# Retention and a two-layer block on one core: w1 in eight pieces, half runs of the first product, and another order of the early work

## The chip, the cores and the metric

The kernel runs on one core of one Trainium2 chip. The time is device microseconds of that core, the median of several executions. A profiled execution of its own gives the trace; its time, its span and the median are told apart below. TensorE is called PE here, its weight loads PEld, VectorE DVE, ScalarE ACT, GpSimd POOL and SyncE SP.

## The reference, cut to what matters

```python
# q, k, v: (B, H, S, D) = (4, 8, 768, 64)
gamma = 1.0 - 2.0 ** (-5.0 - np.arange(H))
for t in range(S):
    state = gamma[None, :, None, None] * state + np.einsum('bhd,bhe->bhde', k[:, :, t], v[:, :, t])
    y[:, :, t] = 1 / np.sqrt(D) * np.einsum('bhd,bhde->bhe', q[:, :, t], state)
x = y.transpose(0, 2, 1, 3).reshape(B, S, H * D)           # 4 x 768 x 512
xn = (x - mean(x)) / np.sqrt(var(x) + 1e-06) * g_ln
out = x + np.maximum(xn @ w_ch1, 0.0) @ w_ch2              # 512 -> 2048 -> 512
```

## The kernel before, in words

There are 24 tiles of 128 tokens: the first chunk of each of the four batches (tiles 0 to 3), then chunks 1 to 5 batch by batch (tiles 4 to 23). Per tile the kernel forms the masked product of q and k (`vis`, `am`), the attention output (`py`), a state that passes from chunk to chunk (`vg`, `pd`, `pb`), the normalisation (`bn`, `xn`, `xc`, `sq`, `rs`), a transpose of the normalised tile (`tx`, `ex`), the first product with relu (`m`, `r`), the second product (`z`), and scale, residual and store (`ad`, `st`). The first product runs over groups of tiles: tiles 0 to 7 each alone, then four groups of two, then two groups of four. A group's product is cut into runs that fill one PSUM bank; `m0_4` is the run of group 0 that begins at hidden block 4 of 16. For a group of one tile such a run is 16 matmuls of 128 columns and needs one quarter of w1; `r0_4` evacuates it with relu.

Nothing schedules this at run time. The list `ORDER` (lines 36 to 96) is the program order, token by token, and each engine works through its own tokens strictly in that order. The letter after a slash names the engine that evacuates or issues the DMA (A is ACT, D is DVE, S is SP), the names after two slashes the PSUM banks: X0 to X3, Y0, Y1, M and PD. An instruction waits until its inputs are there and until its bank or buffer has been read by its last reader; everything behind it on its engine waits too.

The tokens that the steps below touch, with their lines:

- `k1`, `q1`, `v1` (line 337) load one tile of k, q or v and cast it to bf16; `W0` to `W3` (line 356) load a quarter of w1, `Z0` to `Z3` (line 361) a quarter of w2. All of these are issued by POOL, in order, in one queue. Tile 0's k and q come by ACT and SP in float32 (`hk0a` and so on, line 345) and are cast on ACT or DVE (`hkc0`, `hqc0a`, `hqc0b`, line 244/246).
- `iota`, `pos` (lines 265, 270) on POOL, then `small`, `consts`, `zero` (state cleared, line 316), `idn`, `arg`, `lmul`, `cm`, `mask` (line 303) on DVE and `vsc`, `qsc`, `gch` on ACT make the constants.
- `tk2`, `tq2` (line 372) transpose k and q of a tile on PE (tiles 0 to 6), `ek2` (line 244/246) and `eq2` (line 386) evacuate them; from tile 7 on `tr7` transposes by a DMA on SP's queue (line 380) and `eq7` scales.
- `vis2` (line 395), `am2a`, `am2b` (line 408, DVE), `py2` (line 423), `bn2` (lines 431, 432), `xn2` (line 441), `tx2` (line 486), `ex2`.
- `gb` (line 328) broadcasts the gain on PE, `gl` (line 332) takes it to SBUF.
- `warm8_1` (line 564) is 8 matmuls of 512 columns and 1 of 128 on zeros: PE work that computes nothing.

Of the kernel before, what the change touches and what calls it, by code (L numbers as in the profile page):

```python
# [48 lines left out]
ek6/A eq6 r3_12/A pb6 vg6/ vis6//X2,X1 z1_0//M am6a Z2 am6b m4_8//X2 ex5/D Z3 r4_8/A r4_12/A
vg7/ m1_12//X1 py6//Y0 bn6 k9 xn6 rs2 pd6 m5_8//X0 q9 rs4 pb7 rs1 m5_0//X3 tx6//Y1 r5_8/A q8 eq7  # L50
ex6/D m5_4//X2 r5_0/A k8 vg1/ xc6 r1_12/A m5_12//X3 pd7 r5_4/D v8 sq5 vis7//X0,X2 r5_12/D
m6_12//X1 am7b am7a v9 k10 z1_1 pb8 py7 m6_8//X2 bn7 m6_0//X3 z1_2 rs0 xn7a xn7b z1_3 tr9 xc7b
r6_8/A xc7a pd1 tr8 tx7//Y0 z0_0//Y1 ex7/A gv8 ad1 gq8 gk8 z2_0//Y0 k11 gk10 m7_0//X2 z2_1 gk9
q10 q11 gv9 eq9 rs5 rs3 pb9 r7_0/A r6_12/A r6_0/A z2_2 z0_1 gq9 v11 v10 z0_2 vg9/ z0_3 k12 z2_3
ad0 tr10 gq10 z3_0//M v12 gk11 st0/A ad2 z3_1 tr11 eq8 q13 vis8//X2,X1,X3,X0 z3_2 am8b am8a gv10
vg10/ gv11 z3_3 am9a am9b py8 m7_12//X1 bn8 m7_4//X3 ad3 q12 py9 pd9 bn9 gk12 k13 m6_4//X0
z4_0//M xn9a xn8a xn9b gv12 z4_1 xn8b q14 gq11 pb10 z4_2 k15 ex8/S xc9a r7_12/A eq10 z4_3 k14
r7_4/A xc8b sq7 ex9/S vg11/ ad4 pd10 m7_8//X3 gq12 tr12 r7_8/A z5_0//M gq13 v14 pb11 eq11 st1/A
xc8a xc9b z5_1 r6_4/A vg12/ tr13 z5_2 gq14 vg2/ gk13 vis10//X1,X2,X3,X0 am10a z5_3 pd11 am10b
gk15 v13 q15 m8_4//X1 ad5 m8_14//X2 am11a am11b v15 z6_0//M sq6 pb12 gk14 py10 py11 vg14/ bn11  # L60
# [587 lines left out]
```

## Time and profile before

| what | value |
|---|---|
| median of 3 executions | 213.27 us (212.48 to 214.36) |
| profiled execution: its time | 212.35 us |
| profiled execution: its span | 210.5 us |
| mean granted PE clock | 1.00 |
| DVE busy / ACT busy / POOL busy | 127.7 / 76.9 / 96.5 us |
| POOL's load queue (software), share of 16 DMA engines | 84.6% |

The span runs from the first to the last instruction; 1.85 us of the execution's time lie outside it. A row of the timeline gives start, duration, engine, line, operation, output and inputs, and in brackets how long the engine had been idle and what ended that. A row of the chain of waits gives start and duration of one piece of the chain that ended last. PE's busy share must be read with care: matmuls are pipelined, their ends are modelled, and the zero matmuls of line 564 count as busy.

### The profile page before, as it was taken

What the parts mean: (1) busy time and instruction counts of PE and PEld (TensorE: products, weight loads), DVE (VectorE), ACT (ScalarE), POOL (GpSimd) and SP (SyncE); (2) the same over time, 40 slices, a digit from 0 to 9 for tenths busy, and PEclk for the clock granted to TensorE, in tenths of its full rate; (3) what the DMA queues carried; (4) which work ended last, traced back from release to release, by engine and by line L of the source; (5) the groups of instructions that cost most, each with busy time, mean ns of one, the idle gap of its engine ahead of it and who ended that gap; (6) DMA issues with size and microseconds to landing.
All of it is one profiled execution on the core that took longest, in us unless ns stands there. A gap on an engine that the chain in (4) does not pass through costs nothing.

```text
span 210.5 us, 4985 instructions
## 1 busy us (share of the span) xinstructions
PE 204.3 (97%) x2031; PEld 131.8 (63%) x2031; DVE 127.7 (61%) x297; ACT 76.9 (37%) x168; POOL 96.5 (46%) x145
## 2 busy tenths in 40 slices
PE   7898999999999999999999999999999999999994
PEld 2467999897548667676587686475545444444443
DVE  4797889587248878578695566868948402110023
ACT  6265653642400334515237124314281522346000
POOL 8996593495597797780587449500000000000000
PEclk9999999999999999999999999999999999999999
DMA  9999999999999999999999999996032400015005
GB/s 127 172 181 180 163 195 167 125 172 161 159 121 190 123 178 138 150 118 188 225 145 172 170 166 110 137 108 149 1 104 100 101 0 3 0 50 201 0 3 199
DMA packets 109946, 27.11 MB, mean 129 GB/s; under 512 B 102625, under 2 KB 106977, under 8 KB 109922
## 3 DMA queue, kind: packets, MB, share of 16 engines
q0 software_dynamic: 77024, 13.37, 84.6%
q1 hardware_dynamic: 28242, 6.85, 24.0%
q10 hardware_dynamic: 4656, 6.56, 9.7%
q8 instruction: 16, 0.26, 0.5%
q14 instruction: 8, 0.07, 0.1%
HBM read 27.30 MB, written 6.29 MB: 160 GB/s over the span
## 4 chain that ended last, share of the span: by engine, by line
PE 89%; DVE 8%; ACT 1%; issue 1%; DVEq 0%; ACTq 0%
PE X L520 38%; PE M L543 25%; PE Y L543 9%; PE PD L543 4%; PE X L395 3%; PE Y L423 3%; PE PD L465 2%; PE PD L564 2%; DVE trq L386 2%; DVE asb L408 2%; DVE xn L441 1%; PE Y L401 1%; DVE mask L303 1%; PE Y L372 1%; DVE bns L431 1%
## 5 line engine op out<-in xcount | busy, mean ns | idle before, releaser
L520 PE MATMUL X<-xnt,w 128*128 128x128 bf16 (+2 forms) x896 | 93.9, 257 | 0.0
L531 ACT ACTIVATE h<-X 128x512 bf16<-128x512 f32 x89 | 51.2, 602 | 80.6 <-PE X L520 68.7
L520 PEld LDWEIGHTS <-w 128*128 128x128 bf16 x896 | 66.1, 98 | 20.5 <-issue 0.2
L543 PE MATMUL M<-w,h 128*128 128x512 bf16 x256 | 61.5, 379 | 0.0
L543 PEld LDWEIGHTS <-h 128*128 128x128 bf16 x400 | 37.3, 98 | 37.9
L408 DVE TENSOR_TENSOR asb<-X,mask 128x512 bf16<-128x512 f32 x48 | 30.6, 684 | 11.1 <-PE X L395 10.8
L457 POOL TENSOR_TENSOR vg<-v,vsc 128x512 bf16<-128x512 bf16 x20 | 21.3, 1069 | 9.7 <-DMA v<-in_v_dram 8.6
L550 DVE SCALAR_TENSOR_TENSOR osb<-M,rstd,x_all 128x512 f32<-128x512 f32 x16 | 11.9, 746 | 20.4 <-PE M L543 20.0
L447 ACT CAST x_all<-Y 128x256 bf16<-128x256 f32 (+1 forms) x39 | 14.3, 410 | 26.4 <-DVE xn L441 26.4
L337 POOL DMA_DIRECT2D v<-in_v_dram x24 | 21.8, 910 | 3.7 <-DMA w<-in_moe_w_ch_dram 2.5
L431 DVE BATCH_NORM_STATS2 bns<-Y 128x6 f32<-128x256 f32 (+1 forms) x39 | 16.3, 455 | 9.2 <-PE Y L423 9.0
L543 PE MATMUL Y<-w,h 128*128 128x512 bf16 (+1 forms) x96 | 21.8, 370 | 0.0
L441 DVE SCALAR_TENSOR_TENSOR xn<-Y,mv,gb 128x256 bf16<-128x256 f32 (+1 forms) x39 | 18.7, 513 | 1.2 <-PE Y L423 0.6
L475 DVE TENSOR_TENSOR state<-PD,gch 64x256 bf16<-64x256 f32 x40 | 16.6, 415 | 0.6 <-PE PD L465 0.3
L337 POOL DMA_DIRECT2D qk<-in_q_dram x17 | 15.2, 895 | 1.1 <-issue 1.1
L337 POOL DMA_DIRECT2D qk<-in_k_dram x17 | 15.3, 898 | 0.9 <-issue 0.7
L550 DVE SCALAR_TENSOR_TENSOR osb<-PD,rstd,x_all 128x512 f32<-128x512 f32 (+1 forms) x3 | 1.9, 618 | 20.1 <-PE PD L543 20.1
L386 DVE TENSOR_TENSOR trq<-tr,qsc 128x512 bf16<-128x512 bf16 x17 | 10.1, 597 | 3.6 <-DMA tr<-qk 3.4
L366 POOL COPY scrap<-qk 1x1 bf16<-1x1 bf16 x28 | 5.5, 195 | 11.5 <-DMA qk<-in_k_dram 9.7
L564 PE MATMUL PD<-zeros 128*128 128x512 bf16 (+1 forms) x33 | 9.0, 410 | 1.2 <-DVE zeros L250 1.2
L423 PEld LDWEIGHTS <-asb 128*128 128x128 bf16 x192 | 8.0, 98 | 3.5 <-DVE asb L408 1.6
L543 PE MATMUL PD<-w,h 128*128 128x512 bf16 (+1 forms) x48 | 8.8, 326 | 0.0
(75 smaller groups left out, 131.8 us busy)
## 6 DMA issues: line engine op xcount, KB each, us to landing
out_dram<-osb ACTq DMA_DIRECT2D x23, 256.0 KB, 2.4
w<-in_moe_w_ch_dram POOLq DMA_DIRECT2D x8, 512.0 KB, 9.2
v<-in_v_dram POOLq DMA_DIRECT2D x24, 128.0 KB, 6.6
qk<-in_k_dram POOLq DMA_DIRECT2D x17, 128.0 KB, 6.7
qk<-in_q_dram POOLq DMA_DIRECT2D x17, 128.0 KB, 5.5
k<-in_k_dram POOLq DMA_DIRECT2D x6, 128.0 KB, 8.2
q<-in_q_dram POOLq DMA_DIRECT2D x6, 128.0 KB, 7.8
tr<-qk SPq DMA_TRANSPOSE x17, 5.5
```

The costliest lines, as they stand in the source:

```text
L337: nc.gpsimd.dma_start(out=dst, in_=tok[kind][TILES[t]])
L386: nc.vector.tensor_tensor(out=slot(trq, t), in0=x, in1=qsc, op=ALU.mult)
L408: nc.vector.tensor_tensor(out=slot(asb, t)[:, :, par, :], in0=bank(("pa", t, par)).rearrange("p (i t) -> p i t", t=P), in1=mask.rearrange( ...
L423: nc.tensor.matmul(dst, lhsT=slot(asb, t)[:, h // 2, h % 2, :], rhs=v_of(t)[:, h, :], start=(not late and n == H and h == 0), stop=(h >= H ...
L431: nc.vector.bn_stats(out=bns[:, t, i, :], in_=x)
L441: nc.vector.scalar_tensor_tensor(out=dst, in0=src, scalar=mv[:, t, 0:1], in1=g, op0=ALU.subtract, op1=ALU.mult)
L447: nc.scalar.copy(out=dst, in_=src)
L457: nc.gpsimd.tensor_tensor(out=slot(vgs, chunk(t)), in0=v_of(t), in1=vsc[:, c, :].unsqueeze(2).to_broadcast([P, H, D]), op=ALU.mult)
L475: nc.vector.tensor_tensor(out=slot(state, chunk(t) - 1)[o, :, o], in0=pd[o, :, o], in1=gch[o, c - 1, :].unsqueeze(2).to_broadcast([D, NPAI ...
L520: nc.tensor.matmul(bank(("mm", g, ho))[:, j * n * P:(j + 1) * n * P], lhsT=w1[:, ko, (ho + j) * P:(ho + j + 1) * P], rhs=x[:, x0:x0 + n, k ...
L531: nc.scalar.activation(out=dst, in_=src, func=AF.Relu)
L543: nc.tensor.matmul(bank(("m2", t, piece))[:, 0:hi - lo], lhsT=slot(h1, t // 4)[:, ho, t % 4 * P:(t % 4 + 1) * P], rhs=w2[:, ho, lo:hi], st ...
```

## The change

Three things change. `W` takes a half: w1 arrives in eight DMAs of 256 columns (`W0b`, `W0a` and so on) in place of four of 512. `m` takes a half: for tiles 0 to 7 a run of 16 matmuls is emitted as two of 8 that write the two halves of the same bank, at places of their own in the order; the evacuation stays one. And `ORDER` is a new list from the first token to the last. In its early part `q1`, `k1` go ahead of `iota`, `pos`; `zero` and `mask` come earlier; nine loads of k, q and v in place of four go ahead of the first piece of w1; the attention of tiles 0 to 3 goes ahead of the first product; 13 wide zero matmuls (`warm8_1`, `warm1_3`, `warm3_1`, `warm1_2`) stand in place of 22 wide ones; some evacuations change between ACT and DVE (`ek0`, `ek1`, `ek4`, `ek5`, `ek6`, `ex7`, `r0_4`, `r3_0`, `r5_0`, `r1_12` to DVE; `r0_0`, `ex4`, `ex6`, `r5_12` to ACT). The `late` variable in `vis` gives the same start flags as before for the visits that are in use.

```diff
            'osb': 6}}
 
 ORDER = """
-qsc v1 hkc0/A gch hqc0a/D W0 warm8_1 tk0//Y0 hqc0b/A k2 ek0/A warm1_1 tq0//Y1 eq0 q2 mask
-warm1_3 vis0//X1,X2 gb//X3 W1 am0b vg0/ am0a gl v2 warm3_2 tq1//Y1 py0//M tk1//Y0 eq1 ek1/A k3
-bn0 sqt warm3_1 vis1//X3,X0 q3 xn0 v3 am1a xc0 warm2_3 tx0//Y0 am1b ex0/A W2 zero warm3_0 py1//M
-warm1_0 tk2//Y0 pd0 k4 bn1 ek2/A tq2//Y1 q4 m0_0//X3 xn1 eq2 r0_0/D vis2//X1,X2 tx1//Y0 am2a
-am2b m0_4//X0 v4 xc1 ex1/A py2//Y1 k5 r0_4/A m1_4//X1 bn2 q5 tk3//Y0 m1_0//X2 xn2 ek3/A v5
-r1_4/A tq3//M tx2//Y0 xc2 W3 eq3 ex2/D r1_0/A vis3//X0,X1 m2_4//X3 am3a am3b m2_0//X0 pb4 v7
-py3//Y1 r2_0/A sq0 m0_8//X2 bn3 Z0 r2_4/A tk4//M m1_8//X1 xn3 vg4/ k6 ek4/A r0_8/A xc3 tq4//M
-tx3//Y0 eq4 m2_8//X0 r1_8/D ex3/A vg5/ q6 vis4//X2,X3 r2_8/A am4a am4b m3_4//X1 tk5//Y1 tq5//M
-r3_4/D ek5/A pd4 py4//Y0 eq5 k7 m3_0//X0 bn4 q7 vis5//X1,X3 r3_0/A xn4 m3_8//X2 v6 tx4//M
-m0_12//X0 am5b am5a xc4 Z1 sq1 pb5 m2_12//X1 ex4/D py5//Y1 r2_12/D m4_0//X3 bn5 r0_12/A sq4 sq3
-m4_4//X1 xn5 m3_12//X0 r4_0/D xc5 r4_4/A tk6//M pd5 sq2 tx5//Y1 tq6//Y0 tr7 m4_12//X3 r3_8/A
-ek6/A eq6 r3_12/A pb6 vg6/ vis6//X2,X1 z1_0//M am6a Z2 am6b m4_8//X2 ex5/D Z3 r4_8/A r4_12/A
...
-m8_10//X0 r8_6/A rs8 ex10/S eq12 xn11a xc11a vg15/ sq9 xc10a xc11b pb13 eq13 rs6 xc10b z6_3
...
-vis12//X2,X3,X1,X0 q17 v17 gv16 z7_2 am12a gv15 am13a am13b am12b pb14 k18 z7_3 m9_0//X1 ad7
...
-z11_3 gv20 r10_12/A m11_10//X1 vg20/ xn16b ad11 pd19 gq21 r11_10/A z12_0//M m10_14//X0 eq18 tr21
-vg21/ pb20 xn17a eq19 xn17b vg22/ z12_1 r10_14/A xc16b z12_2 sq11 xc16a xc17a xc17b z12_3 k23
-v23 vis18//X3,X0,X1,X2 ad12 ex17/S ex16/S tr22 pd20 am18b z13_0//M am18a z13_1 am19a py18 z13_2
...
-pb21 eq20 ex19/S sq12 xc19a z14_3 tr23 vis20//X1,X2,X0,X3 ad14 pd21 am21a z15_0//M z15_1 eq22
...
-z22_2 z23_0//Y1 z22_3 z20_0//PD z20_1 z20_2 z20_3 z21_3 ad20 ad22 z23_1 st20/A ad21 z23_2 st22/A
-z23_3 st21/A z23b_0//PD ad23 z23b_1 z23b_2 z23b_3 st23/A ad23b st23b/A
+hk0b/A hk0a/S q1 consts small hq0b/A hq0a/S grow table zero touch k1 iota pos v0 q2 k2 idn lmul
+arg cm vsc hkc0/A warm8_1 tk0//Y0 mask hqc0a/D k3 hqc0b/A qsc warm1_3 tq0//Y1 v1 v2 q3 vg0/
+ek0/D gch eq0 warm3_1 tq1//M vis0//X2,X3 eq1 gb//X1 am0b am0a tk1//M sqt gl py0//Y0 ek1/D bn0
+warm1_2 tq2//Y1 W0b eq2 vis1//X1,X0 pd0 W0a xn0 sq0 tk2//Y1 W1a am1b tk3//M ek2/A ek3/A am1a v3
+vis2//X2,X0 xc0 am2b am2a tx0//M W1b py1//Y0 ex0/A k4 bn1 py2//M tq3//Y1 q4 eq3 xn1 vis3//X1,X0
+W2b m0_0b//X3 bn2 tx1//Y1 W2a ex1/A rs0 m0_0a k5 r0_0/A sq1 m1_0b//X2 xn2 am3b am3a sq2 xc2
+tx2//Y1 m1_0a v4 m1_4a//X0 r1_0/A xc1 ex2/D py3//M q5 m2_4a//X1 m2_0a//X3 bn3 m2_0b r2_0/A W3b
+xn3 m2_4b m1_4b rs1 pb4 xc3 sq3 r1_4/A W3a tk4//Y1 m0_4b//X3 ek4/D q6 tq4//Y0 r2_4/A m0_4a eq4
+tx3//M r0_4/D vis4//X2,X0 ex3/A v5 m2_8b//X1 am4a m1_8b//X3 am4b m3_0a//X2 m3_0b k6 m1_8a r3_0/D
+m2_8a tk5//Y1 r1_8/D m0_8b//X2 q7 r2_8/A ek5/D py4//Y0 m3_8a//X3 vg4/ v6 k7 bn4 tq5//M m3_8b eq5
+m0_8a xn4 vis5//X0,X1 pd4 am5a sq4 r3_8/A r0_8/A xc4 m3_4a//X3 tx4//M ex4/A pb5 m3_4b m2_12b//X2
+am5b m2_12a r3_4/D tq6//Y0 m0_12b//X1 eq6 py5//Y1 r2_12/D m4_4b//X3 Z0 Z1 vg5/ bn5 tk6//M m4_4a
+v7 ek6/D r4_4/A xn5 m0_12a vis6//X0,X2 pd5 tr7 Z2 r0_12/A m3_12b//X3 m3_12a am6b rs4 Z3 pb6 am6a
+m4_8b//X2 m1_12b//X1 k8 q9 vg6/ r3_12/A xc5 m1_12a tx5//Y1 ex5/D py6//M rs3 r1_12/D m4_8a
+m5_8b//X3 m5_8a r4_8/A bn6 rs2 xn6 r5_8/A m5_0a//X0 m4_12a//X1 pd6 sq6 sq5 pb7 xc6 m5_12b//X2
+m5_0b tx6//M r5_0/D m4_12b m5_12a ex6/A eq7 z1_0//M vg7/ r4_12/A r5_12/A m6_12a//X3 vis7//X0,X1
+m6_12b z1_1 am7a am7b k9 pd7 rs6 py7 m5_4a//X2 m4_0b//X1 bn7 vg1/ q8 m4_0a xn7b r4_0/D v9 pb8
...
+pb14 ex10/S m8_0//X0 ad6 q16 m8_4//X3 xc11b r8_0/A eq12 tr15 z7_0//M r8_4/A st5/A st1/A
+vis12//X2,X3,X1,X0 z7_1 am13a am13b am12a m8_8//X1 am12b z7_2 k18 gv16 q17 r8_8/A z7_3 gk16 gq15
...
+xn14b q20 eq17 eq18 pd17 m10_2//X0 m9_14//X1 xc15b r9_6/A k20 ad9 pb18 eq16 sq11 ex15/S ex14/S
...
+am16a gk20 gq20 gv19 gq21 am17a py16 py17 m10_12//X1 m10_8//X0 r10_12/A ad10 bn17 gk21 eq19
...
+z11_3 z12_2 ad11 z12_3 vg22/ vis18//X3,X0,X1,X2 ad12 pd20 am18b am18a z13_0//M st7/A st12/A
...
+xc19a r11_12/A pb21 eq20 rs12 z14_2 ex18/S z14_3 vis20//X1,X2,X0,X3 ad14 tr22 pd21 am21a
...
+z21_2 z22_3 st20/A st18/A ad19 z21_3 ad22 z23_0//PD ad21 z23_1 st21/A st19/A z23_2 st22/A z23_3
+z23b_0//M ad23 z23b_1 z23b_2 z23b_3 st23/A ad23b st23b/A
 """.split()
 
 
@@ -351,8 +353,9 @@
         evacuate(eng, dst[:, hs], raw(kind)[:, hs])
 
     @on("W")
-    def _(eng, j):
-        s = slice(j * DM, (j + 1) * DM)
+    def _(eng, j, half=None):
+        s = slice(j * DM, (j + 1) * DM) if half is None else slice((2 * j + half) * DM // 2,
+                                                                   (2 * j + half + 1) * DM // 2)
         nc.gpsimd.dma_start(out=w1[:, :, s], in_=w1_v[:, :, s])
 
     @on("Z")
@@ -388,6 +391,7 @@
     @on("vis")
     def _(eng, first):
         ts = visit[first]
+        late = [t for t in ts if t >= T0]
         for t in ts:
             for i in range(NPAIR):
                 for par in range(2):
@@ -395,12 +399,12 @@
                     nc.tensor.matmul(bank(("pa", t, par))[:, i * P:(i + 1) * P], lhsT=kT(t)[o, i, :],
                                      rhs=slot(trq, t)[o, i, :], start=True, stop=True)
         for t in ts:
-            for i in range(NPAIR if t >= T0 else 0):
+            for i in range(NPAIR if t in late else 0):
                 for par in range(2):
                     o = slice(D * par, D * (par + 1))
                     nc.tensor.matmul(
                         y_of(t, par)[:, i * D:(i + 1) * D], lhsT=slot(trq, t)[o, i, :],
-                        rhs=slot(state, chunk(t) - 1)[o, i, o], start=(i == 0 and t == ts[0]), stop=False,
+                        rhs=slot(state, chunk(t) - 1)[o, i, o], start=(i == 0 and t == late[0]), stop=False,
                         skip_group_check=True)
 
     @on("am")
@@ -513,9 +517,9 @@
         nc.vector.reciprocal(out=rstd[:, s], in_=rstd[:, s])
 
     @on("m")
-    def _(eng, g, ho):
+    def _(eng, g, ho, half=None):
         n, (x, x0) = GROUPS[g], xnt_of(g)
-        for j in range(4 // n):
+        for j in range(4 // n) if half is None else (2 * half, 2 * half + 1):
             for ko in range(KO):
                 nc.tensor.matmul(bank(("mm", g, ho))[:, j * n * P:(j + 1) * n * P],
                                  lhsT=w1[:, ko, (ho + j) * P:(ho + j + 1) * P],
@@ -597,10 +601,13 @@
             m = re.fullmatch(r"(\d+)([ab]?)", arg)
             return EMIT[kind], (int(m.group(1)), letter[m.group(2)])
         if kind in ("m", "r"):
-            g, ho = map(int, arg.split("_"))
-            if kind == "m":
+            m = re.fullmatch(r"(\d+)_(\d+)([ab]?)", arg)
+            g, ho = int(m.group(1)), int(m.group(2))
+            if kind == "m" and where:
                 at(("mm", g, ho))
-            return EMIT[kind], (g, ho)
+            return EMIT[kind], (g, ho) + ((letter[m.group(3)],) if kind == "m" else ())
+        if kind == "W":
+            return EMIT[kind], (int(arg[0]), letter[arg[1:]])
         if kind in ("z", "ad", "st"):
             m = re.fullmatch(r"(\d+)([abc]?)(?:_(\d))?", arg)
             t, piece = int(m.group(1)), "abc".index(m.group(2) or "a")
```

## The prediction, made before the change was run

> **What bounds the kernel now.** I read the page, then the chain of waits and PE's timeline stage by stage, then DVE's timeline of the first 35 us, then the landing of every load. The page:
>
> ```profile
> PE 204.3 (97%) x2031; PEld 131.8 (63%) x2031; DVE 127.7 (61%) x297; ACT 76.9 (37%) x168; POOL 96.5 (46%) x145
> ...
> PE 89%; DVE 8%; ACT 1%; issue 1%; DVEq 0%; ACTq 0%
> ```
>
> PE is the bound over the span, but its 204.3 us hold zero matmuls and modelled ends. So I counted PE by start-to-start times, which do not overlap: a transpose of a tile 0.22 us, `vis` of an early tile 0.33, `py` 0.23 (0.45 with state), a run `m` 0.89 for one tile (0.87 and 0.86 for groups of two and four), a quarter of `z` 0.86, `gb` 1.05. All of the order's useful PE work comes to 192.5 us, and none of it changes. I call "lost" the start of a PE token minus the useful work before it. It is 12.5 us at `vis3` (21.50 - 8.97), 12.95 at `m4_8` (40.16 - 27.21), 13.9 at `vis18`, 14.6 behind it, 14.9 at the end; 3 us of last evacuation and store follow. So the kernel is full from 22 us on, and 12.5 of the 18 us that are not PE work lie ahead of that. The chain there:
>
> ```profile
> 6.99 1.89 DVE mask L303
> ...
> 8.97 1.30 DVE asb L408 x2
> ...
> 10.76 0.71 DVE bns L431
> ...
> 11.79 0.75 DVE xn L441
> 12.54 1.20 DVE asb L408 x2
> 13.74 0.27 DVE state L316
> ...
> 15.37 0.75 DVE xn L441
> 16.12 0.33 DVE trq L386
> 16.45 0.60 DVE h L533
> 17.05 1.21 DVE asb L408 x2
> ...
> 21.50 0.40 PE X L395 x8
> ```
>
> From 7 to 18 us DVE is the bound, not PE: mask, masked products, normalisation, clearing, relu follow each other without a gap. PE fills the time with zeros (first row of its timeline, then the last wait of the trace that PE feels, in DVE's rows):
>
> ```profile
> 1.19 3.70 PE L564 MATMUL PD<-zeros 128*128 128x512 bf16 x9 [1.19 <-DVE zeros L250]
> ```
>
> ```profile
> 130.86 2.27 DVE L386 TENSOR_TENSOR trq<-tr,qsc 128x512 bf16<-128x512 bf16 x1
> 133.06 0.47 DVE L441 SCALAR_TENSOR_TENSOR xn<-Y,mv,gb 128x256 bf16<-128x256 f32 x1
> ```
>
> The nine zero matmuls take 0.43 us each; from 6.8 us on a 512-column matmul takes 0.216. `eq19` takes 2.27 us in place of 0.42 beside two `vg` on POOL (130.81 to 132.84), and `xn17`, `xc17` behind it hold the Y banks that `vis18` needs: 0.74 us of PE.
>
> **The change, part by part.** *Loads.* By the landings that the trace records, loads of one tile land 0.88 us apart and a quarter of w1 2.55 us after its predecessor (20.43 to 22.95, 28.03 to 30.60), back to back until 56 us. A tile is 1024 packets of 128 bytes over 16 DMA engines (13.8 ns of an engine each), a quarter 512 packets of 1024 bytes (80 ns). A half is 512 packets of 512 bytes: between half a quarter's time, 1.27 us, and a whole quarter's, 2.55 (same packet count). The line through the two rows gives 42 ns, 1.34 us; I take that, since the short packets cost so little. All of w1 then costs 8 x 1.34 - 4 x 2.55 = +0.5 us of queue, at worst +10. With the first load issued at 0.83 (where `iota` stood) and 5.2 us to land: q1 6.1, ninth load 13.1, W0b 14.5, W0a 15.8, W1a 17.1, v3 18.0, W1b 19.4, W2b 22.6, W3b 28, k7 35, Z0 37.6. [...]
>
> *Issues.* Four more `W` issues of 0.79 us and two moved loads of 0.9 us stand on POOL. The two delay `iota`, `pos`, hence `idn`, `arg`, `cm`, `vsc`, by 1.9 us. `zero` (0.82 us, out of the chain at 13.74) fills that on DVE. Mask then starts at 4.5 instead of 6.9 and ends at 6.45; `hqc0a` is behind it (6.75, was 5.2), so `tq0` 6.75 (5.8), `vis0` 8.1 (7.0), `am0` 8.65 to 9.9 (8.97 to 10.27).
>
> *The DVE chain.* Steps by the starts above: `am` 0.6, `bn` with aggregate 0.96, `xn` 0.67, `eq` 0.33, PSUM copy 0.35, relu 0.6. From `am0` to the end of `am3`: eight `am` 4.8, three `bn` 2.9, three `xn` 2.0, two `eq` 0.7, `ek1` 0.35, `rs0` 0.1 = 10.9, with the short waits on PE 11.2: `am3` ends at 19.8. Before it was 23.1. What left this stretch is `zero`, `r0_0` (now ACT), `ex1`; what joined is `ek1`.
>
> *PE's order.* Attention of four tiles comes first, so the first product is late: with `eq3` at 16.2, `vis3` starts at 16.2 and `m0_0b` at 16.6; before it was 14.9. Then `m0_0a` 17.3 (its piece landed 15.8), a wait of 0.4 for `ex1`, `m1_0`, `m1_4a` 19.35 (W1a 17.1), `py3` 19.9, a short wait for `ex2` behind `am3`, `m2_4`, `m2_0`, `m1_4b`, `tk4` at 22.5. Useful work ahead of `tk4`: 11 transposes 2.45, four `vis` 1.32, four `py` 0.93, `gb` 1.05, `pd0` 0.22, ten half runs 4.45 = 10.42. Lost: 12.1, against 12.5 before. Splitting the runs costs nothing: same matmuls, one evacuation.
>
> *From 22 to 43 us.* DVE's tokens from `ek0` to `r2_12`: 12 `am` 7.3, five `bn` 4.8, five `xn` 3.4, seven `eq` 2.3, five copies 1.75, five relu 3.0, two `pb` 1.7, `rs` 0.2 = 24.4 us. From 6.75 that ends at 31.2 at the earliest; PE, at 21.4 us of useful work with 12.5 lost, needs it at about 33.9. DVE may idle 2.7 us there. Stepping on, token by token, I find one more PE wait: `vis6` 0.35 for `ek6`, which stands behind `bn5`, with `pd5`, `m3_12` and all of PE queued behind it. At `z1_0` lost is 12.5 (before, 12.95 at the nearest rows). Z0 at 37.6 and tr7 (k7 at 35, its DMA took 4.5) at 39.5 are ahead of their need at 43. So the front gives -0.45.
>
> *Later.* `eq18`, `eq19` stand 22.7 and 11.7 us of PE work ahead of `vis18` (2.6 before), so the 0.74 us go. Late next may be `eq12`, 0.8 us of PE ahead of `vis12` (3.7 before), or `eq20`, 1.7 ahead of `vis20`; one of them beside a `vg` costs up to 1.85 (2.27 - 0.42). I give back 0.5. The end, `z23`, `z23b` and their stores, is the same: 0. Sum: -0.45 - 0.74 + 0.5 = -0.7. The profiled execution, 212.35 (span 210.5 and 1.85 around it), would be 211.65; the median was 0.9 above that execution, so I predict **212.6**, own range 211.2 to 214.2, chance 0.48.
>
> **The rivals.** *DVE becomes the bound (slower).* DVE's allowance of 2.7 us is smaller than the 3.7 us it idled on PE and ACT between 6 and 35 us before (`trq` 2.5, `bns` 0.8, `asb` 0.4). From an idle time of 2.7 us on each further microsecond goes to PE; my step-by-step walk uses about all of it, and 5 us would cost 2.3: 214.9, to 216 with stalls at `ek`, `eq` (DVE takes over six PSUM copies from ACT and gives back two; in all it has 3.4 us more work). Chance 0.17. *The clock (slower).* PE computes from 9.4 to 16.6 only some 3.5 of 7.2 us, with 13 wide zero matmuls instead of 22. Before, full pace came 5.6 us after the first matmul, with pauses under 0.3 us; now there is one of 0.65 at 6.1. If the slow pace lasts 5 us from `tq0`, 3.9 us of work up to `vis1` takes twice as long, about 1 of it in gaps: +2.5, 215.1. No row shows a half-idle PE losing the clock. Chance 0.17. [...] *The pieces land late (slower).* At 2.55 us each W0a lands at 18.2, W1a 20.8, W1b 24.2, W3a near 39 against 32 needed: up to +7, 219; against it, the packet rows. Chance 0.05. *Faster.* Lost is 11.3 at `m0_0b`; if PE then waits for nothing and the later stalls stay away, -1.2 - 0.5 more: 210.9. Against it, `ex1`, `ex2`, `ek6` each sit behind 1 to 2 us of DVE or ACT work. Chance 0.13.
>
> **How the numbers follow.** Within 1% of 213.27, about what a measurement tells from no change, means 211.1 to 215.4. Likeliest case 0.48: 0.04 faster, 0.42 same, 0.02 slower. DVE 0.17: 0.04 same, 0.13 slower. Clock 0.17: 0.08 same, 0.09 slower. Late pieces 0.05 slower, the faster case 0.13 faster. Together 0.17, 0.54, 0.29. The range 210.4 to 216.5 takes in the faster case, the DVE and clock cases, and leaves out the late pieces and the far ends.
>
> **What would show it.** Right: first X matmul of line 520 near 16.6, mask at 4.5, `am3` ended near 20, lost 12 to 12.6 at `tk4`, w1's pieces 1.3 to 1.4 us apart, no PE wait at `vis18`. DVE rival: PE idle behind `trk`, `trq`, `xnt` between 22 and 43 us with DVE above 95% busy. Clock rival: matmuls of 128 columns at more than 0.06 us apart after 8 us. Late pieces: PE's weight loads of line 520 waiting on `w`. I am wrong if PE idles over 1 us anywhere after 45 us.

## The result, and the profile after

| what | before | after |
|---|---|---|
| median, taken together on one chip | 213.81 us (4 executions) | 223.23 us (4 executions, 221.56 to 224.57) |
| ratio to before | | 1.0439, interval 1.0338 to 1.0540 |
| profiled execution: time / span | 212.35 / 210.5 us | 221.56 / 219.8 us |
| mean granted PE clock | 1.00 | 0.984 |

The change makes the kernel slower by 4.4%, 10.6 us above the forecast of 212.6 and far outside its range. From the page of the changed kernel, the two lines that the prediction shows of the page before, and between them the granted clock in 40 slices of 5.5 us (in tenths of full speed):

```profile
PE 204.1 (93%) x1992; PEld 133.3 (61%) x2018; DVE 128.3 (58%) x303; ACT 75.2 (34%) x162; POOL 99.5 (45%) x149
...
PEclk9996999996999999999999999999999999999999
...
PE 69%; DMA 16%; DVE 6%; POOL 4%; issue 1%; ACT 1%; POOLq 0%; DVEq 0%; ACTq 0%; SPq 0%
```

The busy times are nearly those of before. What is new is a chain of waits in which DMA has 16% (it did not appear before), and two dips of the clock, in the slices that begin at 16.5 and 49.5 us. "Lost" time, counted as the prediction did (start of a PE token minus the useful work before it), shows where it comes in:

| stretch | lost before | lost after | difference |
|---|---|---|---|
| up to `vis4` | 12.65 | 13.86 | +1.21 |
| `vis4` to `vis7` | 0.42 | 4.66 | +4.24 |
| `vis7` to `vis12` | 0.44 | 2.05 | +1.61 |
| `vis12` to `vis16` | 0.26 | 3.06 | +2.80 |
| `vis16` to `z23b` | 1.14 | 0.56 | -0.58 |
| sum | 14.91 | 24.19 | +9.28 |

The two profiled times differ by 9.21 us, so the table holds all of it. PE's own rows at these places (line 399 is `vis`, 427 `py`, 524 `m`, 547 `z`):

```profile
14.52 0.41 PE L427 MATMUL M<-v,asb 128*128 128x64 bf16 x8 [0.63 <-DVE asb L412]
...
15.66 0.40 PE L399 MATMUL X<-trq,trk 64*128 64x128 bf16 x8 [0.52 <-DVE trq L389]
16.98 0.90 PE L524 MATMUL X<-xnt,w 128*128 128x128 bf16 x8 [0.92 <-DMA w<-in_moe_w_ch_dram]
...
50.64 0.40 PE L399 MATMUL X<-trq,tr 64*128 64x128 bf16 x8 [4.22 <-DVE trq L389]
...
103.10 1.02 PE L547 MATMUL M<-w,h 128*128 128x512 bf16 x4 [1.63 <-DVE osb L554]
...
123.53 1.02 PE L547 MATMUL M<-w,h 128*128 128x512 bf16 x3 [0.85 <-DVE osb L554]
```

The largest is `vis7`. PE names DVE, but DVE's rows name what DVE itself waited for:

```profile
50.16 0.43 DVE L389 TENSOR_TENSOR trq<-tr,qsc 128x512 bf16<-128x512 bf16 x1 [5.44 <-DMA tr<-qk]
...
102.30 0.75 DVE L554 SCALAR_TENSOR_TENSOR osb<-M,rstd,x_all 128x512 f32<-128x512 f32 x1 [3.60 <-DMA out_dram<-osb]
...
119.53 3.29 DVE L389 TENSOR_TENSOR trq<-tr,qsc 128x512 bf16<-128x512 bf16 x2
122.74 0.74 DVE L554 SCALAR_TENSOR_TENSOR osb<-M,rstd,x_all 128x512 f32<-128x512 f32 x1
```

`eq7` waits for the transpose `tr7`. It was issued at 36.83 us, as soon as k7 had landed (36.75), and landed at 50.14: 13.3 us, against 4.5 before (38.54 to 43.04). At 102.30 `ad7` waits for a store: the change puts `st1` right ahead of `vis12`, it is issued at 95.17 and landed at 102.20, and `ad7` may not overwrite its buffer before; `z8` needs the bank that `ad7` reads. The place is only half of it: the page's median for a store of this size is 2.5 us from issue to landing, and this one took 7.0. At 2.5 it would have landed at 97.7, ahead of 98.70, where `ad7`'s wait begins. At 119.53 `eq17` and `eq18` take 3.29 us together, and `ad9` behind them holds the bank of `z10`. POOL's rows show what stood beside `tr7` (first two rows) and beside `eq17`, `eq18` (last row):

```profile
35.33 1.51 POOL L364 DMA_DIRECT2D w<-in_moe_w_ch_dram  x2
...
49.18 1.04 POOL L461 TENSOR_TENSOR vg<-v,vsc 128x512 bf16<-128x512 bf16 x1 [9.51 <-DMA v<-in_v_dram]
...
120.47 2.06 POOL L461 TENSOR_TENSOR vg<-v,vsc 128x512 bf16<-128x512 bf16 x2
```

The first row is `Z2` and `Z3`, issued ahead of the transpose. Before, POOL stood blocked there, by accident: `vg6` waited for its v, and `Z2`, `Z3` behind it were issued only at 40.48, when the transpose was half done:

```profile
39.49 1.04 POOL L457 TENSOR_TENSOR vg<-v,vsc 128x512 bf16<-128x512 bf16 x1 [6.06 <-DMA v<-in_v_dram]
40.48 1.55 POOL L361 DMA_DIRECT2D w<-in_moe_w_ch_dram  x2
```

The clock, by stretches of the changed kernel (after the stretch: its length, busy us and instructions of PE, PEld, DVE, ACT, POOL, then the granted clock, the DMA engines' busy share and GB/s):

```profile
10.34:13.75 3.41, 2.78 (x46) 1.99 (x44) 3.38 (x7) 2.14 (x5) 3.41 (x5) 1.00 2.57 151
13.75:17.16 3.41, 1.35 (x29) 0.98 (x25) 3.34 (x10) 0.30 (x1) 3.41 (x5) 1.00 1.16 138
...
17.20:20.50 3.30, 3.24 (x33) 2.98 (x31) 1.87 (x3) 1.65 (x5) 2.21 (x4) 0.50 1.86 176
...
46.30:51.30 5.00, 0.78 (x23) 0.70 (x21) 0.67 (x2) 0.00 (x0) 2.11 (x3) 1.00 1.35 135
51.30:54.70 3.40, 3.40 (x28) 2.30 (x26) 1.30 (x4) 0.00 (x0) 3.40 (x4) 0.50 1.24 87
```

Twice PE idles, and twice the next 3.41 us run at half pace (17.16 to 20.57 and 51.29 to 54.70). The first time PE waited 0.63 and 0.52 us for DVE and 0.92 for the first piece of w1, and was busy for only 1.35 of 3.41 us; the second time it is the wait for `tr7`.

### The profile page after: what moved, and what is told of

The parts are those of the page before. It is cut to its first block, busy times and chain, and to the rows that moved or that the text cites. A ratio compares the mean times of both kernels' runs of the same rounds, so it can differ in the third digit from the quotient of the medians.

```text
span 219.8 us, 4928 instructions
## 1 busy us (share of the span) xinstructions
PE 204.1 (93%) x1992; PEld 133.3 (61%) x2018; DVE 128.3 (58%) x303; ACT 75.2 (34%) x162; POOL 99.5 (45%) x149
## 4 chain that ended last, share of the span: by engine, by line
PE 69%; DMA 16%; DVE 6%; POOL 4%; issue 1%; ACT 1%; POOLq 0%; DVEq 0%; ACTq 0%; SPq 0%
PE X L524 26%; PE M L547 22%; PE Y L547 9%; DMA tr<-qk 6%; PE PD L547 4%; DMA w<-in_moe_w_ch_dram 4%; DMA out_dram<-osb 3%; DMA qk<-in_k_dram 3%; PE X L399 2%; PE Y L427 2%; DVE trq L389 2%; PE PD L469 2%; POOL k L339 1%; DVE bns L435 1%; POOL q L339 1%
## 5 line engine op out<-in xcount | busy, mean ns | idle before, releaser
L524 PE MATMUL X<-xnt,w 128*128 128x128 bf16 (+2 forms) x896 | 95.5, 260 | 1.0 <-DMA w<-in_moe_w_ch_dram 0.9
L524 PEld LDWEIGHTS <-w 128*128 128x128 bf16 x896 | 67.9, 99 | 21.9 <-DMA w<-in_moe_w_ch_dram 1.4
L547 PE MATMUL M<-w,h 128*128 128x512 bf16 (+1 forms) x237 | 59.1, 373 | 3.7 <-DVE osb L554 2.5
L554 DVE SCALAR_TENSOR_TENSOR osb<-M,rstd,x_all 128x512 f32<-128x512 f32 (+1 forms) x16 | 11.6, 722 | 19.4 <-PE M L547 15.8
L547 PE MATMUL Y<-w,h 128*128 128x512 bf16 x92 | 22.1, 379 | 0.1
L435 DVE BATCH_NORM_STATS2 bns<-Y 128x6 f32<-128x256 f32 (+1 forms) x38 | 15.4, 443 | 5.3 <-PE Y L427 5.1
L445 DVE SCALAR_TENSOR_TENSOR xn<-Y,mv,gb 128x256 bf16<-128x256 f32 (+1 forms) x38 | 17.5, 498 | 1.0 <-ACT x_all L451 0.8
L554 DVE SCALAR_TENSOR_TENSOR osb<-Y,rstd,x_all 128x512 f32<-128x512 f32 x6 | 4.5, 750 | 20.3 <-PE Y L547 18.5
L547 PE MATMUL PD<-w,h 128*128 128x512 bf16 (+1 forms) x46 | 10.2, 361 | 0.1
L399 PE MATMUL X<-trq,tr 64*128 64x128 bf16 x136 | 5.4, 217 | 4.2 <-DVE trq L389 4.2
## 6 DMA issues: line engine op xcount, KB each, us to landing
w<-in_moe_w_ch_dram POOLq DMA_DIRECT2D x4, 512.0 KB, 13.5
```

The costliest lines, as they stand in the source:

```text
L435: nc.vector.bn_stats(out=bns[:, t, i, :], in_=x)
L445: nc.vector.scalar_tensor_tensor(out=dst, in0=src, scalar=mv[:, t, 0:1], in1=g, op0=ALU.subtract, op1=ALU.mult)
L524: nc.tensor.matmul(bank(("mm", g, ho))[:, j * n * P:(j + 1) * n * P], lhsT=w1[:, ko, (ho + j) * P:(ho + j + 1) * P], rhs=x[:, x0:x0 + n, k ...
L547: nc.tensor.matmul(bank(("m2", t, piece))[:, 0:hi - lo], lhsT=slot(h1, t // 4)[:, ho, t % 4 * P:(t % 4 + 1) * P], rhs=w2[:, ho, lo:hi], st ...
L554: nc.vector.scalar_tensor_tensor(out=slot(osb, t + piece)[:, 0:hi - lo], in0=bank(("m2", t, piece))[:, 0:hi - lo], scalar=rstd[:, t:t + 1] ...
```

## The experiments

The theory after the result: the new order fills the load queue while `tr7` is in flight, so the transpose is late and PE loses 4.2 us there and 1.6 us more to the half pace behind it; an early clock drop, the store and the `vg` beside `eq17` make up the rest; halves and half runs cost nothing. The rival: the halves (more DMAs, split runs) or the order as a whole cost it, in many places. The diffs below show the token list, with banks and evacuating engines left out.

**Holding Z2 and Z3 until tr7 has landed.** Of the changed kernel; `hold7` is a copy of one element of `tr7` on POOL.

```diff
-vis6 pd5 tr7 Z2 r0_12 ... rs4 Z3 pb6 ... m1_12b k8 q9 vg6 r3_12
+vis6 pd5 tr7 r0_12 ... rs4 pb6 ... m1_12b vg6 hold7 Z2 Z3 k8 q9 r3_12
```

> The changed kernel; POOL reads one element of the transposed tile 7 before it issues Z2, Z3, k8 and q9, so that these loads come only after the DMA transpose tr7 has landed. Theory (the transpose shares the DMA engines packet by packet with a full load queue): tr7 lands 4 to 9 us after its issue in place of 13.3, PE's wait of 4.4 us at vis7 and the half clock behind it (1.4 us) go, and the time falls by 4.5 to 6 us, to about 217.5 to 218.7. Rival (tr7 is slow for another reason, its inputs or its own queue): it still takes about 13 us, and the time stays within 1 us of 223.2 or rises, as Z2 and Z3 come later.

`tr7` took 8.56 us and PE did not wait at `vis7`. But `vg7` now stood behind the hold, so `pd7` waited 1.54; `z8` waited 2.72 for the store; and the clock fell there too. Four executions spread from 213.98 to 221.76 us, too wide for a ratio; their median, 219.47, lies above the 217.5 to 218.7 that was expected. The wait goes with its cause; the total was left to the later runs.

**The reverse: filling the queue in the kernel before.**

```diff
-... xc4 Z1 sq1 ... am6a Z2 am6b ... ex5 Z3 r4_8 ... bn6 k9 xn6 ... q9 rs4
+... xc4 Z1 Z2 Z3 k9 q9 sq1 ... am6a am6b ... ex5 r4_8 ... bn6 xn6 ... rs4
```

> The kernel before; POOL issues Z2, Z3, k9 and q9 ahead of the vg6 that waits for v6, so that the load queue is full while tr7 runs. Nothing else moves. Theory: tr7 takes 9 to 14 us in place of 4.5, PE waits 2 to 5 us at vis7, with the half clock behind it, and the time rises by 2 to 6 us to 216 to 220. Rival (the slow transpose belongs to something else in the change): tr7 stays at 4 to 6 us and the time within 1 us of before.

Ratio 1.0253 (1.0195 to 1.0311). `tr7` took 10.48 us. PE's rows in this kernel:

```profile
48.51 0.21 PE L395 MATMUL X<-trq,tr 64*128 64x128 bf16 x1 [1.86 <-DVE trq L386]
49.56 0.58 PE L395 MATMUL X<-trq,tr 64*128 64x128 bf16 x7 [0.84 <-DVE h L533]
```

Half pace followed from 48.75 to 55.58. Lost time went from 12.5 at `vis4` to 19.1 at `vis12` (12.65 to 13.5 before): four loads issued some 7 us earlier cost the kernel before 2.5%, with nothing else of the change in it.

**The halves alone.** The changed code, with the order of before, each `W` and `m` written as its two halves side by side.

```diff
-W0 ... m0_0//X3 ... W1 ...
+W0a W0b ... m0_0a//X3 m0_0b ... W1a W1b ...
```

> The kernel before with the code of the change and the order of before: each quarter of w1 as two halves side by side, each run of tiles 0 to 7 as two half runs side by side. Theory (the order, not the halves, made the change slow): a half lands 1.3 to 1.4 us after its predecessor, and the time stays within 1 us of before. Rival (halving costs, by the number of packets or of DMAs): pieces 2 us or more apart and the time 2 us or more above before.

Ratio 1.0032 (0.9994 to 1.0069), no difference; the pieces landed 1.31 to 1.35 us apart, `tr7` took 4.43. The halves are not the cause.

**Zero matmuls against the early clock drop.** Of the changed kernel; 15 zero matmuls of 512 columns in PE's pauses between 11 and 17 us.

```diff
-tk2 ... vis2 ... py1 ... py2 ... vis3 W2b m0_0b
+heat1 tk2 ... heat3 vis2 ... heat1 py1 ... heat3 py2 ... heat3 vis3 heat4 W2b m0_0b
```

> The changed kernel with 15 more zero matmuls of 512 columns in PE's pauses between 11 and 17 us, into bank X3, which is free then. Theory (the pauses let the clock fall for 3.4 us at 17.2): the granted clock stays at full pace up to the wait at vis7, the runs m0_0 and m1_0 take half the time, and PE's lost time at m1_0a is 1.0 to 1.4 us less; the time falls by 0.8 to 1.4 us if nothing behind takes it back. Rival (DVE or the pieces of w1 pace this stretch): the clock stays up, and lost time at m1_0a falls by under 0.5 us. Third: the clock falls all the same.

The clock held until 51.7, yet nothing was won: ratio 1.0547 (1.0453 to 1.0641). At full pace PE ran into the next pieces of w1:

```profile
18.74 1.07 PE L524 MATMUL X<-xnt,w 128*128 128x128 bf16 x16 [0.54 <-DMA w<-in_moe_w_ch_dram]
...
21.23 0.62 PE L524 MATMUL X<-xnt,w 128*128 128x128 bf16 x8 [0.75 <-DMA w<-in_moe_w_ch_dram]
```

In this profile W1a landed at 21.18 (19.65 in the changed kernel's), so part of it may be that execution's; lost at `vis4` was 14.54. The wait at `vis7` was 5.5 us, `tr7` took 13.3, and `z8` lost 3.3 behind the store, so this run says nothing against the other causes.

**The store of tile 1 behind that of tile 2**, of the changed kernel, one execution: `st1` moved from behind `st5` to behind `st2`.

```diff
-r7_12 st2 m7_4a ... st5 st1 vis12
+r7_12 st2 st1 m7_4a ... st5 vis12
```

> The changed kernel with the store of tile 1 issued right behind that of tile 2 (some 15 us earlier) in place of behind tile 5's. Theory (DVE's ad7 needs the output buffer that the late store of tile 1 still reads, and holds bank M against z8): ad7 waits for no store, PE's wait of 1.8 us at z8 goes to under 0.3 us; time 1.5 to 2 us less if the runs were alike. Rival (z8 waits for something else that is late at that place): a wait of over 1 us stays at z8.

217.73 us. `ad7` no longer waits for a store, nor `z8` for it (lost 19.48 there, 19.46 at `vis12`):

```profile
98.84 0.75 DVE L554 SCALAR_TENSOR_TENSOR osb<-M,rstd,x_all 128x512 f32<-128x512 f32 x1 [1.25 <-PE M L547]
```

How long the store takes decides too. In four profiles `st1` stands at its late place, and lost time from `vis12` to `z8` grows with the store's time from issue to landing: 0.3 us where it took 5.6 (the next run), 1.8 where it took 7.0 (the changed kernel), 2.7 at 7.9 (the hold), 3.3 at 8.6 (the zero matmuls). The row of the next run:

```profile
99.47 0.75 DVE L554 SCALAR_TENSOR_TENSOR osb<-M,rstd,x_all 128x512 f32<-128x512 f32 x1 [2.12 <-DMA out_dram<-osb]
```

So the order made the store matter, and its slowness in that execution set the price. Why it is slow there was not tested; in the kernel before, a store issued at 92.90 took 6.9 us too, and nothing waited for it.

**eq17 and eq18 behind ad9**, of the changed kernel, one execution.

```diff
-q20 eq17 eq18 pd17 ... ad9 pb18 eq16
+q20 pd17 ... ad9 pb18 eq17 eq18 eq16
```

> The changed kernel with eq17 and eq18 behind ad9 on DVE in place of ahead of it. Theory (one of them took 2.96 us in place of 0.42 beside two vg on POOL, and ad9 behind it held bank M): PE's wait of 1.0 us at z10 falls under 0.3 us; an eq may still take 1 to 3 us, now off PE's path. Rival: z10 waits as before, for another engine.

217.76 us; no wait at `z10`. With the last 0.25 us of a `vg` beside them, by POOL's rows, the two take 0.89 us together, where they took 3.29:

```profile
118.29 0.89 DVE L389 TENSOR_TENSOR trq<-tr,qsc 128x512 bf16<-128x512 bf16 x2
```

In both executions `tr7` took 11.5 us and the wait at `vis7` was 3.1 and 3.4, so their totals hold some luck as well, the second also by the shorter store. The second profile also kept the full clock at 16.38, with the same early order. Its row for the stretch that decides:

```profile
12.97:16.38 3.41, 2.20 (x42) 1.81 (x41) 3.38 (x8) 0.89 (x2) 3.41 (x5) 1.00 1.27 157
```

Lost at `vis4` is 13.86, 14.03 and 13.89 where the clock fell (the changed kernel, the runs with `st1` moved and with the hold), and 12.50, 12.26 and 12.35 where it did not (this run and the two mended ones below). Part of that may be the landing of w1's first piece: with the same place in the order, and its issue at 10.75, it landed at 15.03 in this run and at 16.93 in the changed kernel's profile. The fair pair is the run with the hold (half pace from 14.51 to 21.34) and the second mended run, with landings at 16.30 and 16.22: the drop costs 1.5 us there.

2.20 us busy out of 3.41 kept the pace; 1.35 (above) and 1.47 (with `st1` moved) lost it. But these runs give no threshold: with the hold the clock fell at 14.51 after a stretch with 2.26 us busy, and with all three mended it held after 2.26 (11.57 to 14.98) and after 1.51 (45.70 to 49.11). In the changed kernel's trace the clock changes at 17.16, 20.57, 51.29 and 54.70 us, one, nine and one stretches of 3.41 us apart, and the one that decides starts elsewhere in each of three executions (12.97 here, 13.22 with `st1` moved, 13.75 in the changed kernel's); that the same early order falls on one side or the other because of this is my reading. The half-paced stretches are 3.41 us long in the changed kernel, and 6.83 with the hold (14.51 to 21.34) and with the queue filled in the kernel before (48.75 to 55.58).

**All three mended**: hold, store and `eq`.

> The changed kernel with three mends at once: loads held behind tr7, the early store of tile 1, eq17 and eq18 behind ad9. Theory (those three waits and the clock's fall behind the first make the loss, and the early part costs about 1 us): 9.4 us of added lost time become 0.5 to 1.5, time 0 to 1.5 us above before (ratio 1.00 to 1.01). Rival (the order as a whole is slower, and others waits come up where these go): 3 us or more above before.

Ratio 1.0133 (1.0082 to 1.0184), profiled 213.28 us. `tr7` took 7.72, lost at `vis4` was 12.26, and no wait was left at `vis7`, `z8` and `z10`. The clock was full in this execution; in the other five its mean was 0.983 to 0.992. What took the waits' place is `vg7` behind the hold:

```profile
48.60 0.38 PE L473 MATMUL PD<-vg,qk 128*128 128x128 bf16 x4 [1.90 <-POOL vg L465]
```

**The hold behind vg7, and v7 ahead of Z0**, against the run above.

```diff
-m4_4b Z0 Z1 vg5 ... v7 ek6 ... m1_12b vg6 hold7 Z2 Z3 k8 q9 ... z1_0 vg7
+m4_4b v7 Z0 Z1 vg5 ... ek6 ... m1_12b vg6 vg7 hold7 Z2 Z3 k8 q9 ... z1_0
```

> The changed kernel with three places of its order mended: the load of v7 ahead of Z0, and Z2, Z3, k8, q9 held on POOL until tr7 has landed (with vg6, vg7 ahead of that hold); the store of tile 1 behind that of tile 2; eq17 and eq18 behind ad9. My theory (the loss behind 45 us is the late tr7 with its half-pace clock, the store ahead of ad7, and eq17 beside vg): tr7 takes 6 to 9 us, no PE wait above 0.5 us at vis7, pd7, z8 and z10, lost about 14 at the end where the kernel before has 14.9, ratio 0.99 to 1.01. Rival (the new order is worse in many small places spread over the rest): ratio 1.02 or more with these waits gone. Rival (the early clock drop returns): half pace between 14 and 21 us, +1.4 us, ratio 1.005 to 1.015.

Ratio 1.0119 (1.0056 to 1.0181). The profiled execution had full clock all through and yet took 214.31 us, so the last rival, the early drop, does not explain this one. It is not out for the median: the other five executions show a mean granted clock of 0.992 (four) and 0.976, and by the profiles one half-paced stretch of 3.41 us takes some 0.008 off the mean (0.984 with two in the changed kernel). Where those stretches lay was not profiled. `tr7` took 6.78, and the waits at `vis7`, `pd7`, `z8`, `z10` are gone. But `Z2`, held back, now lands at 49.61, too late for `z1`:

```profile
49.65 1.02 PE L551 MATMUL M<-w,h 128*128 128x512 bf16 x3 [1.08 <-DMA w<-in_moe_w_ch_dram]
```

This execution also lost 1.8 us near 129 us, behind a late transpose of a later tile; the next run, with the same order there, did not.

**The same with zero matmuls, vg0 behind W1b and pd0 behind m0_0a.** The other four groups of zero matmuls stand as in the run with them above.

```diff
-q3 vg0 ... vis1 pd0 W0a xn0 sq0 tk2 ... W1b py1 ... rs0 m0_0a k5
+q3 ... vis1 W0a xn0 sq0 heat1 tk2 ... W1b vg0 heat1 py1 ... rs0 m0_0a pd0 k5
```

> The kernel of the run above, with 15 zero matmuls in PE's pauses between 11 and 17 us, and vg0 moved behind the fourth piece of w1 on POOL, so that W0b is issued about 1 us earlier. Theory (the early stretch is set by the landing of w1's pieces, and the clock falls because PE is half idle there): full clock from 7 us on, W0b lands about 16.0 in place of 16.9, m0_0b starts 0.6 to 0.9 us earlier, lost at vis4 about 11.7 to 12.3, ratio 0.985 to 1.0. Rival (the zero matmuls cost what they save): W1a still lands at 19.6 or later, m1_4a waits for it, lost at vis4 13 or more, ratio as the run above or higher.

Median 213.26, ratio 1.0046 (1.0008 to 1.0084); profiled 211.97, lost 14.6 at the end (14.91 before). W0b landed at 16.01, but the four zero matmuls ahead of `m0_0b` ended only at 17.1, and lost at `vis4` was 12.59: the early gain expected did not come. Ten of its twelve executions have a mean clock of 0.998 or more, against one of six in each of the two mended runs above, so the gain on them may well be the clock; `vg0` moved with it, and the share of each was not measured. With the named causes mended, the new order is within half a per cent of the old one.

**Small packets in front of tr7**, in the kernel before: k9, q9, q8, k8 go ahead of `Z2`, `Z3`, and all six ahead of `vg6`.

```diff
-xc4 Z1 sq1 ... Z2 ... Z3 ... k9 ... q9 ... q8 ... k8
+xc4 Z1 k9 q9 q8 k8 Z2 Z3 sq1 ...
```

> The kernel before, with k9, q9, q8, k8 and then Z2, Z3 issued ahead of vg6, so that the load queue is as full beside tr7 as in the run where Z2, Z3 stood first, but with small 128-byte packets in front. Theory A (the transpose's 256-byte packets take turns with the queue's packets, so the size of those decides): tr7 takes 5 to 7 us, wait at vis7 under 1 us. Theory B (any full load queue slows it alike): tr7 takes 9 us or more, wait at vis7 1.5 us or more, as with Z2, Z3 in front (10.48 us, 2.03 us).

Ratio 1.0357 (1.0283 to 1.0431), no better than with `Z2`, `Z3` in front: `tr7` took 12.17 us, as theory B has it. DVE's row:

```profile
49.22 0.43 DVE L386 TENSOR_TENSOR trq<-tr,qsc 128x512 bf16<-128x512 bf16 x1 [4.99 <-DMA tr<-qk]
```

I then counted the packets of these traces (`tr7` has 1024 packets of 256 bytes):

| kernel | issue to first packet, us | first to last packet, us | load packets of 128 / 1024 bytes in between |
|---|---|---|---|
| before | 1.28 | 2.64 | 0 / 46 |
| halves alone | 1.29 | 2.62 | 0 / 116 |
| mended, vg7 ahead of the hold | 3.53 | 2.77 | 0 / 168 |
| Z2, Z3 early | 3.94 | 5.84 | 1179 / 553 |
| small packets in front | 4.52 | 6.98 | 958 / 533 |
| after | 3.95 | 8.25 | 1162 / 825 |

So a full queue costs twice: the first packet comes 2.3 to 3.2 us later, and the rest goes two to three times as slowly. In the mended run of the table, where the hold keeps `Z2` and `Z3` out, only the first of the two is left. It was no clean test of the size: 533 packets of 1024 bytes ran beside the transpose all the same. The packets of the two queues stand mixed: of the 3011 that the table counts for the changed kernel, in order of their starts, 861 follow one of the other queue. And the load queue is slowed in turn: in the changed kernel Z1 landed at 43.63 and v7, one tile, 5.4 us behind it (0.88 elsewhere).

**Is DVE the bound from 7 to 18 us?** The kernel before with mask ahead of the cast of tile 0's q and the clearing right behind it:

```diff
-hkc0 gch hqc0a W0 ... eq0 q2 mask warm1_3 ... W2 zero warm3_0
+hkc0 gch mask hqc0a zero W0 ... eq0 q2 warm1_3 ... W2 warm3_0
```

> The kernel before with one part of the change alone: mask goes ahead of tile 0's q cast and zero follows it, both some 2.5 and 7 us earlier than before; loads, products and stores as before. Theory A (DVE sets the early chain, as the chain of waits says): lost time at vis3 falls by 0.8 to 1.9 us, ratio 0.992 to 0.997. Theory B (the loads set it, DVE only looks busy): lost time at vis3 falls by less than 0.4 us, ratio 0.998 to 1.002.

Ratio 0.9981 (0.9946 to 1.0016): nothing. Lost time was 0.8 us less at `tx0`, and 11.69 again at `m0_4` (11.68 before), which started at 17.09 in both. The second quarter of w1 landed at 17.04 in both. PE's row in this run:

```profile
17.09 1.07 PE L520 MATMUL X<-xnt,w 128*128 128x128 bf16 x16 [0.63 <-DMA w<-in_moe_w_ch_dram]
```

The run with small packets in front shows the reverse. Up to `xc4` its order is that of before, but in its profile the second quarter landed at 15.66: `m0_4` started at 15.91, and lost at `vis4` was 11.50 in place of 12.65, with DVE's order untouched.

**Both at once**: this order with the halves side by side.

> The order of the kernel before with two things at once that each changed nothing alone: the halves of w1 (side by side), whose second quarter then lands near 16.0 instead of 17.04, and mask ahead of the cast of tile 0's q with the clearing behind it, which starts DVE's chain about 0.8 us earlier. Theory (DVE and the landing of w1 bind the stretch from 7 to 20 us together, each hiding the other): m0_4 starts about 16.3 in place of 17.09, lost at vis4 11.7 to 12.1 in place of 12.65, ratio 0.995 to 0.998. Rival (a third thing, such as v2 or v3 still to come in the same queue, holds PE there): lost at vis4 12.4 or more, ratio 0.999 to 1.004.

Ratio 0.9993 (0.9960 to 1.0026), lost 12.22 at `vis4`: between the two theories' numbers, and in the time the rival's. PE's rows show one load after the other:

```profile
16.89 0.62 PE L525 MATMUL X<-xnt,w 128*128 128x128 bf16 x8 [0.28 <-DMA w<-in_moe_w_ch_dram]
17.85 0.39 PE L428 MATMUL Y<-v,asb 128*128 128x64 bf16 x8 [0.35 <-DMA v<-in_v_dram]
```

W1b landed at 16.84 and v2 at 17.81. In the kernel before, v2 landed at 17.97 and `py2` started at 18.01. The load queue binds this stretch, piece after piece; in the last run below PE waited 1.9 us there for v2 alone.

**vg21 and vg22 away from eq19**, in the kernel before, and the same on top of the run above (the last run):

```diff
-tr21 vg21 pb20 xn17a eq19 xn17b vg22 z12_1 ... k23 v23 vis18
+tr21 pb20 xn17a eq19 xn17b z12_1 ... k23 v23 vg21 vg22 vis18
```

> The kernel before, with vg21 and vg22 moved on POOL from ahead of k23 to behind v23, so that eq19 has no vg beside it. Theory (eq19 is held by vg, and xn17, xc17 behind it hold the Y banks that vis18 needs, 0.74 us of PE; that the changed kernel lost this wait is its one lasting gain): eq19 takes 0.42 us in place of 2.27, xn17 ends by 131.9 in place of 133.5, PE's wait between vis18's two halves goes, ratio 0.9955 to 0.998. Rival (another cause sets vis18, the landing of tr19 or xc17's own length): eq19 short, PE's wait there stays above 0.3 us, ratio 0.999 to 1.003.

> The kernel of the run above with vg21 and vg22 behind v23 as well. Theory (the two gains lie apart in time and add up): ratio 0.990 to 0.995. Rival (the early gain does not exist, only that of the vg stays): ratio 0.995 to 0.999.

0.9959 (0.9922 to 0.9995) and 0.9960 (0.9924 to 0.9996): the only kernels whose interval lies below 1, and the early part adds nothing. DVE's rows of the first:

```profile
132.20 0.97 DVE L386 TENSOR_TENSOR trq<-tr,qsc 128x512 bf16<-128x512 bf16 x1
133.09 0.47 DVE L441 SCALAR_TENSOR_TENSOR xn<-Y,mv,gb 128x256 bf16<-128x256 f32 x1
```

`eq19` takes 0.97, 2.27 before (why not 0.42 is not shown: by POOL's rows `vg20` had ended at 132.16), and PE no longer waits beside `vis18`: lost grows by 0.12 from `vis18` to `vis20`, by 0.86 before. In the kernel before, three `eq` with both inputs in SBUF overlap a `vg` for over 0.1 us and take 0.73 us (0.44 us of overlap), 1.28 (0.99) and 2.27 (2.02); the other fourteen take at most 0.43. So does the one at 26.36, which reads a PSUM bank, wholly beside the `vg` at 25.91.

## Why the prediction was wrong

**The step that failed** is "Z0 at 37.6 and tr7 (k7 at 35, its DMA took 4.5) at 39.5 are ahead of their need at 43". k7 landed at 36.75, 1.8 us late, and that alone would have cost nothing: with 4.5 us more `tr7` lands at 41.3, and PE came to wait for it at 46.4. The 4.5 us were the error: that row was taken where the load queue had all but run out (46 load packets between the first and the last of the transpose), and the change refills the queue at just this place (1987 packets). I priced the loads of that stretch by their own landings, and took the transpose's time as given. `tr7` measured 13.3 us. It cost 4.2 us of PE directly and 1.6 through the half pace behind it (second and third row of the table), 5.9 of 9.3. The reverse edit in the kernel before and the hold show this, not only the trace.

**The early part.** Its steps on the compute engines held: mask started at 5.04 (4.5 predicted), `am0` ran from 8.40 to 9.7 (8.65 to 9.9), `am3` ended at 19.1 (19.8), `vis3` started at 15.66 (16.2). The pieces came 1.3 to 1.4 us apart, as read from the two rows, so the rival of 2.55 us for each fell, and the halves and half runs cost nothing. Two sizes were off. The ninth load landed at 13.73 (13.1 predicted) but W0b at 16.93 (14.5): POOL does `vg0` between the two issues, and the piece took 6.2 us from issue to landing; I had spaced it by the queue alone. How much of this is `vg0` is open, since with `vg0` in place the same piece landed anywhere from 15.03 to 17.32 in other executions. And the clock, a rival at 0.17, did fall: I wrote "No row shows a half-idle PE losing the clock"; now one does. It costs about 1.5 us here, not 2.5. Without the drop lost is 12.26 to 12.50 at `vis4`, against 12.65 before, so the forecast of a small early gain held but for that, with some luck: the pieces came later than forecast and `vis3` earlier.

**DVE as the bound from 7 to 18 us** was a misreading. DVE was indeed without a gap there, but shifting it earlier gave nothing, because `m0_4` starts 0.05 us after its quarter lands and `py2` 0.04 us after v2 does. I had both landings and did not lay them beside PE's starts. The DVE rival, built on this, did not occur.

**Later.** The wait beside `vis18` went, worth 0.74 as predicted. "I give back 0.5" for `eq12` or `eq20` had the right mechanism and the wrong token: it was `eq17`, 1.0 us. The store was not looked at: I followed loads and evacuations through the new order, and not the `st` tokens with the buffers that they free, nor how long a store takes at that place. That is 1.8 us. "I am wrong if PE idles over 1 us anywhere after 45 us" names just what happened, twice.

**What stays open.** The mended versions are still 0.5 to 1.3% above before; their profiled executions show waits at changing places (`z1`, a later transpose), which I did not follow further, and most of the other executions of the first two have a mean clock below full, which was not profiled. At which busy share the clock falls, and why a piece of w1 issued at the same time lands up to 2.3 us apart from one execution to another, stays open too. Why the first packet of a transpose comes 2.3 to 3.2 us later when the queue is full was measured and not explained.

## What to carry to other kernels

A DMA's duration in a trace holds only for what was queued beside it (`tr7` took 4.5 us beside 46 load packets, 13.3 beside 1987): before a load is moved earlier, list the transfers in flight at its new place, and those that it used to leave alone because its queue was blocked. To find what binds a stretch, lay the landing of each load beside the start of its first user; an engine without gaps can still be slack (DVE from 7 to 18 us: moving its chain earlier gave a ratio of 0.9981). When a list is reordered, follow the stores too, with the time that one takes at its new place, and put no operation like `eq19` (two SBUF inputs, 2.27 us beside two `vg` on POOL, 0.42 away from them) where something waits behind it.

## What the runs showed of the hardware

- A DMA transpose on SP's queue took 4.4 to 4.5 us from issue to landing with 46 or 116 load packets between its first and last packet, and 10.5 to 13.3 with 1491 to 1987; a load of one tile behind it landed 5.4 us after the one before, 0.88 elsewhere.
- A store of 256 KB took 5.6 to 8.6 us from issue to landing around 95 us in four profiles of the new order, where the page's median is 2.5.
- The granted clock fell to half after a stretch of 3.41 us in which PE was busy for 1.35, 1.47 and once 2.26 us, and held after others with 1.51, 2.20 and 2.26. Half pace lasted 3.41 or 6.83 us each time.
- Eight loads of 256 KB cost about the same queue time as four of 512 KB: 1.31 to 1.35 us apart against 2.55.
